# Spreading one expert's partial products over TensorE's four column groups, in a fused attention and soft-MoE kernel

## The chip, the cores and the metric

The kernel runs on one core of a Trainium2 chip. A core has TensorE (PE; its weight loads are listed apart as PEld), VectorE (DVE), ScalarE (ACT), GpSimd (POOL) and SyncE (SP), each with an instruction queue of its own that it works through in order, and 16 DMA engines that carry the transfers which SP and POOL issue. Matmuls write to PSUM; ScalarE and VectorE read it, GpSimd doesn't. The metric is the device time of one execution in microseconds (us). Inputs and output lie in HBM as float32.

## What is computed

Chunk-selected causal attention (4 batches, 8 heads, 768 positions, head size 64), whose output is the input of a soft mixture of experts: 3072 rows of 512 columns, 8 experts with 4 slots each, hidden size 1024. What matters here is the second part, cut from the reference:

```python
logits = x @ phi                                  # 3072 x 32
d = exp(logits - logits.max(0)); d /= d.sum(0)
slot_input = (d.T @ x).reshape(E, 4, 512)
for e in range(E):
    slot_out[e] = relu(slot_input[e] @ w1[e]) @ w2[e]
c = exp(logits - logits.max(1)); c /= c.sum(1)
return c @ slot_out.reshape(32, 512)
```

Every slot's output needs all rows of x, so nothing can be written before the last expert is done.

## The kernel before

**The loop.** 16 pairs of heads (4 per batch) are worked through by the loop from L570, i = 1 to 15; the order on each engine is the order in which the code issues the instructions. In step i stand the scores of pair i in six groups (`scores`, TensorE; L297 and L307), their exponentials (`expo`, ScalarE, L321) with causal masks (`mask`, GpSimd, L331), the products with v of pair i-1 (`pv`, L349), the normalisation and transposes of pair i-2 (L362, L371), and preparations for pairs i+1 and i+2 (transposes of k and q L205, bounds L256, selection L268). Scores have two PSUM buffers (`p_sc`), so ScalarE can be at most two groups behind TensorE.

**Loads.** All loads go through GpSimd's queue and are cast to bf16 on the way: k and q of pair i+4 (L145), v of pair i+2 (L150) and the sixteen expert matrices of 1 MB each (L138), spread over the steps by `wplan`. The last of the sixteen is w2 of expert 7.

**The MoE's part of the loop.** When the four pairs of a batch are done, the steps i = 6, 10 and 14 do that batch's share. Its combine weights are made in `moe_comb` (GpSimd, L457) and `moe_comb2` (L460): two exponentials on ScalarE write them to `c_pad`, a tile of 128 partitions x 6 row tiles x 4 groups x 32 columns. Expert e = 4g + j has columns 4g to 4g+3 of group j; columns 8 to 31 of each group stay zero from a memset at the start. `moe_ct` (L485) transposes `c_pad` on TensorE, six transposes (L488), and VectorE copies the result into `cT_all` (L496). In a step the order on GpSimd is: masks of groups 2 and 3, loads of k and q, rescaling of `si_acc` (`moe_scale`, L448, not for the first batch), load of v, load of a weight matrix, masks of group 4. On ScalarE the two exponentials of `moe_comb2` stand between the exponentials of groups 4 and 5. On TensorE `moe_ct` stands behind the last products with v of the step and ahead of the next step's scores.

**The tail.** The last batch's share follows from L653 on, with the same pieces. `experts_in` (L760) and `hidden_T` (L775) make the hidden layer. Slot outputs are summed in PSUM, `so_ps`, two halves of 256 columns each; group j (32 partitions) belongs to experts j and 4+j. `experts_out` (L795) multiplies: expert e uses one column group of TensorE, 32 columns of weights, so that matmuls of four experts can run side by side. Expert 7 comes last, alone. ScalarE copies both halves into `so_sb`, scaled by 1 over the column sums of d (`zinv`, from `zrow`); then `cT_all` times `so_sb` gives the output rows, which VectorE and ScalarE scale by 1 over the row sums of c (`cinv`, from `col_sums`, L679) on their way from PSUM, and SP stores them. The first 512 rows are made and stored in column halves (`half_out`, L827), the other 2560 at full width in pieces of 256 rows.

Of the kernel before, what the change touches and what calls it, by code (L numbers as in the profile page):

```python
# [10 lines left out]
F32 = mybir.dt.float32  # L11
BF16 = mybir.dt.bfloat16
ALU = mybir.AluOpType
ACT = mybir.ActivationFunctionType
# [4 lines left out]
CH = 32  # L19
NCHUNK = 24  # L20
NQT = 6
P = 128
# [38 lines left out]
def kernel(  # L61
# [23 lines left out]
    static = ctx.enter_context(tc.tile_pool(name="static", bufs=1))  # L85
# [13 lines left out]
    c_pad = static.tile([P, NQT, 4, CH], BF16, name="c_pad")  # L99
# [3 lines left out]
    w_sb = []  # L103
# [5 lines left out]
    ones_sq = static.tile([P, P], BF16, name="ones_sq")  # L109
# [4 lines left out]
    squad = static.tile([P, 2, 2, NCHUNK], BF16, name="squad")  # L114
    schunk = static.tile([P, 2, NCHUNK, 1], BF16, name="schunk")
    headsel = static.tile([P, 1, 2, 1], BF16, name="headsel")
    ns_t = [static.tile([P, NJ, 2, 2, CH], BF16, name=f"ns_t{i}") for i in range(2)]

    small = ctx.enter_context(tc.tile_pool(name="small", bufs=1))
# [43 lines left out]
        nc.vector.memset(t[:, :, :, D:D + 1], 1.0)  # L163
    for h in range(2):
        nc.vector.memset(headsel[h * 64:(h + 1) * 64, :, h, :], 1.0)

    nc.gpsimd.affine_select(
        out=squad, in_=squad, compare_op=ALU.not_equal, fill=NEG, base=0,
# [3 lines left out]
        out=squad, in_=squad, compare_op=ALU.not_equal, fill=-1.0, base=-NCHUNK,  # L172
# [5 lines left out]
        out=qgrp, in_=qgrp, compare_op=ALU.not_equal, fill=1.0, base=0,  # L178
# [3 lines left out]
        out=caus[:4], in_=caus[:4], compare_op=ALU.is_ge, fill=NEG, base=0,  # L182
# [277 lines left out]
    def moe_comb2(b):  # L460
        lc = st.pop(("lc", b))
        for g in range(2):
            nc.scalar.activation(
                c_pad[:, :, :, g * SPE:(g + 1) * SPE],
                lc[:, :, g * 16:(g + 1) * 16].rearrange("p t (j s) -> p t j s", j=4), func=ACT.Exp,
            )

    def moe_dispatch(b):
        d_sb = st.pop(("d", b))
        x = st.pop(("x", b)).rearrange("p t h d -> p t (h d)").rearrange("p t (a c x) -> p t a x c", a=NDG // 2, x=2)  # L470
        si = p_tp.tile([P, NDG + 1, NS], F32, name="si_ps", tag="tp")
        for dg in range(NDG + 1):
            for t in range(NQT):
                nc.tensor.matmul(
                    si[:, dg, :], lhsT=x[:, t, dg // 2, dg % 2, :] if dg < NDG else ones_sq,
                    rhs=d_sb[:, t, :], start=(t == 0), stop=(t == NQT - 1),
                )
        if b == 0:
# [173 lines left out]
    hT_pad = pads.tile([P, NFG, E, CH], BF16, name="hT_pad")  # L652
# [26 lines left out]
    def col_sums(ps, b):  # L679
        c = cT_all[:, b * NQT:(b + 1) * NQT].rearrange("p (m a) (c x) -> p m x (a c)", a=2, x=2)  # L680
        for n in range(NQT):
            nc.tensor.matmul(
                ps[:, n:n + 1], lhsT=c[:, n // 2, n % 2], rhs=ones_sq[:, :1], start=True, stop=True)

    csa = h_ps[0][:, 1, :BL * NQT]
    for b in range(BL):
# [18 lines left out]
    def cinv(n):  # L705
        return inv_a[:, n:n + 1] if n < BL * NQT else inv_b[:, 1 + n - BL * NQT:2 + n - BL * NQT]
# [4 lines left out]
        lg2, lhsT=mneg.broadcast_to([NS, P]), rhs=rep.broadcast_to([NS, NQT, NS]), start=False, stop=True,  # L711
# [3 lines left out]
        bc, lhsT=mneg.broadcast_to([NS, P]), rhs=identf[:NS, :NS], start=True, stop=True,  # L715
# [13 lines left out]
    for g in range(2):  # L729
        nc.scalar.activation(  # L730
            c_pad[:, :, :, g * SPE:(g + 1) * SPE],
            lc[:, :, g * 16:(g + 1) * 16].rearrange("p t (j s) -> p t j s", j=4), func=ACT.Exp,
        )
    keep(2)
    moe_dispatch(BL)
    keep(2)
# [2 lines left out]
    zrow = tail.tile([1, 4, CH], F32, name="zrow")  # L739
# [8 lines left out]
    for g in range(2):  # L748
        sl = slice(g * 16, (g + 1) * 16)
        nc.vector.tensor_tensor(  # L750
            zrow[:, :, g * SPE:(g + 1) * SPE],
            si_acc[:1, NDG, sl].rearrange("p (j s) -> p j s", j=4),
            si[:1, NDG, sl].rearrange("p (j s) -> p j s", j=4), op=ALU.add,
        )
    zinv = inv_b[:, :1]
    cT = cT_all.rearrange("p (m a) (c x) -> p m x (a c)", a=2, x=2)

    h_sb = tail.tile([P, 2, 512], BF16, name="h_sb")
    so_sb = [tail.tile([P, Dm // 2], BF16, name=f"so_sb{y}") for y in range(2)]
# [31 lines left out]
    HD = Dm // 2  # L791
    so_t = p_at.tile([P, 2, 512], F32, name="so_ps0", tag="at")
    so_ps = [so_t[:, 0, :HD], p_sc.tile([P, HD], F32, name="so_ps1", tag="sc")]

    def experts_out(fs, es, ys):  # L795
        for y, f in ((y, f) for y in ys for f in fs):
            for fg in range(f * 4, (f + 1) * 4):
                for e in es:
                    g, j = divmod(e, 4)
                    nc.tensor.matmul(  # L800
                        so_ps[y][j * CH:(j + 1) * CH, :], lhsT=hT_pad[:, fg, e, :],
                        rhs=w_sb[E + e][:, fg * Dm + y * HD:fg * Dm + (y + 1) * HD],
                        start=(g == 0 and fg == 0), stop=(g == 1 and fg == NFG - 1),
                    )

    experts_in(0, 0)
    moe_ct(B - 1)
# [3 lines left out]
    hidden_T(0)  # L811
    experts_in(1, 1)
    relu(1)
    NM, NH = B * NQT // 2, 2
    homes = {"sc": p_sc, "tp": p_tp, "at": p_at}
    half_homes = [iter("tp at sc tp".split()), iter("sc tp sc tp".split())]

    def rows(m):
        return out[m * 2 * P:(m + 1) * 2 * P, :].rearrange("(p x) d -> p x d", x=2)

    def scaled(x, o, ps, n):
        if x == 0:
            nc.vector.tensor_scalar_mul(o, ps, cinv(n))  # L823
        else:
            nc.scalar.activation(o, ps, func=ACT.Copy, scale=cinv(n))

    def half_out(m, y):  # L827
        o_sb = op.tile([P, 2, HD], F32, name="oh_sb", tag="oh_sb", bufs=2 * NH)
        for x in range(2):
            tag = next(half_homes[y])  # L830
            o_ps = homes[tag].tile([P, HD], F32, name="oh_ps", tag=tag)
            nc.tensor.matmul(o_ps, lhsT=cT[:, m, x], rhs=so_sb[y], start=True, stop=True)
            scaled(x, o_sb[:, x, :], o_ps, 2 * m + x)
            if m == y == 0:
                nc.sync.dma_start(out=rows(m)[:, x, :HD], in_=o_sb[:, x, :])
        if m + y > 0:
            nc.sync.dma_start(out=rows(m)[:, :, y * HD:(y + 1) * HD], in_=o_sb)

    w_ctx.close()
    op = ctx.enter_context(tc.tile_pool(name="op", bufs=5))  # L840
    experts_out([0], range(4), [0, 1])
    hidden_T(1)
    sums()
    experts_out([1], range(4), [0, 1])
    experts_out([0, 1], [4, 5, 6], [0, 1])
    experts_out([0, 1], [7], [0])
    nc.scalar.activation(so_sb[0], so_ps[0], func=ACT.Copy, scale=zinv)
    experts_out([0], [7], [1])
    half_out(0, 0)
    experts_out([1], [7], [1])  # L850
    nc.scalar.activation(so_sb[1], so_ps[1], func=ACT.Copy, scale=zinv)
    half_out(1, 0)
    for m in range(NH):
        half_out(m, 1)

    n = 0
    for m in range(NH, NM):
        o_sb = op.tile([P, 2, Dm], F32, name="o_sb", tag="o_sb")
        for x in range(2):
            tag = ("at", "sc", "tp", "sc", "tp")[n % 5]  # L860
            o_ps = homes[tag].tile([P, Dm], F32, name="o_ps", tag=tag)
            for y in range(2):
                nc.tensor.matmul(  # L863
                    o_ps[:, y * HD:(y + 1) * HD], lhsT=cT[:, m, x], rhs=so_sb[y], start=True, stop=True)
            scaled(x, o_sb[:, x, :], o_ps, 2 * m + x)
            n += 1
            if m == NM - 1:
                nc.sync.dma_start(out=rows(m)[:, x], in_=o_sb[:, x, :])
        if m < NM - 1:
            nc.sync.dma_start(out=rows(m), in_=o_sb)  # L870
# [30 lines left out]
```

## Time and profile before

| | |
|---|---|
| median of three runs | 166.99 us (166.96 to 167.58) |
| the profiled execution | 166.89 us, its span 165.2 us |
| busy share of the span: PE, DVE, ACT, POOL | 86%, 73%, 74%, 62% |
| moved on GpSimd's queue | 26.25 MB (bf16), read from HBM as float32 |
| stored on SP's queue | 6.29 MB |

How the lines are read: "start us, us, engine line op out<-in ... xcount [idle before <-releaser]" is one row of a timeline: when the first of the merged instructions started, how long from there to the end of the last, and, in brackets, how long the engine stood idle before it and what ended that. L331 is line 331 of the kernel. In the chain of waits a row is a stretch of the path that ended last. A row of windows has, for each engine, the busy time in that stretch and in brackets the number of instructions, then TensorE's granted clock (1.00 is full), the busy share of the DMA engines and GB/s. The page's strips cut the span into 40 slices of 4.13 us; digits are tenths. A busy TensorE isn't TensorE at its peak, since matmuls are pipelined.

### The profile page before, as it was taken

The numbers are of one execution on the slowest core, as the hardware profiler recorded it, in microseconds if no ns is written. First come the engines' busy times: TensorE is split into PE (matmuls) and PEld (weight loads), VectorE is DVE, ScalarE is ACT, GpSimd is POOL, SyncE is SP. The second block draws the span as 40 slices with busy tenths as digits, with TensorE's granted clock in tenths as the row PEclk, the third lists the DMA queues.
The fourth block names the chain that finished last, engine by engine and source line by source line (L and its number), as shares of the span: only waits on it lengthen the run. The fifth ranks groups of instructions, "written<-read, shape, count | busy, mean of one in ns | idle before, by whom it ended". The sixth has DMA issues, their size and how long they took to land.

```text
span 165.2 us, 6132 instructions
## 1 busy us (share of the span) xinstructions
PE 142.8 (86%) x2541; PEld 97.6 (59%) x2541; DVE 119.9 (73%) x419; ACT 122.8 (74%) x166; POOL 103.1 (62%) x202
## 2 busy tenths in 40 slices
PE   7986779999999898999999899998989999894500
PEld 2353456766767585677768567675868747552200
DVE  3376988989999979989997999898536521083620
ACT  3668879999999798999989699996886311193510
POOL 6978749979889398878949796768936200000000
PEclk9999999999999999999999999999999999999655
DMA  3999999999999999999999999999999999158995
GB/s 46 148 157 171 207 157 106 171 192 201 203 200 204 201 205 181 211 193 183 209 191 212 193 214 193 208 219 197 203 207 217 211 215 192 28 195 326 408 404 197
DMA packets 41132, 32.94 MB, mean 199 GB/s; under 512 B 26384, under 2 KB 35600, under 8 KB 41104
## 3 DMA queue, kind: packets, MB, share of 16 engines
q0 software_dynamic: 38416, 26.25, 108.0%
q1 hardware_dynamic: 2688, 6.29, 9.9%
q8 instruction: 20, 0.33, 0.7%
q14 instruction: 8, 0.07, 0.1%
HBM read 52.49 MB, written 6.29 MB: 356 GB/s over the span
## 4 chain that ended last, share of the span: by engine, by line
PE 31%; DMA 29%; ACT 18%; DVE 9%; issue 5%; POOL 4%; DVEq 0%; ACTq 0%
DMA w_sb<-in_moe_w_dram 14%; ACT e_sb L321 11%; DMA k_in<-in_k_dram 9%; DMA out_dram<-o_sb 6%; PE sc_ps L297 6%; PE at_ps L349 4%; PE tr_ps L205 4%; PE sc_ps L307 4%; PE warm_ps L197 4%; ACT qT L214 4%; PE xT_ps L371 2%; DVE mx L268 2%; PE ub_ps L256 2%; DVE x_sb L362 1%; POOL e_sb L331 1%
## 5 line engine op out<-in xcount | busy, mean ns | idle before, releaser
L321 ACT ACTIVATE e_sb<-sc_ps 128x1024 bf16<-128x1024 f32 (+1 forms) x96 | 83.1, 917 | 8.1 <-PE sc_ps L307 7.7
L331 POOL TENSOR_SCALAR_AFFINE_SELECT e_sb<-e_sb 128x256 bf16<-128x256 bf16 x96 | 38.4, 419 | 16.2 <-ACT e_sb L321 15.6
L297 PE MATMUL sc_ps<-qT,kT 64*128 64x384 bf16 (+3 forms) x258 | 36.8, 305 | 2.7 <-ACT e_sb L321 1.7
L307 PE MATMUL sc_ps<-nsT,smask 64*128 64x384 bf16 (+2 forms) x294 | 38.1, 284 | 0.1
L349 PE MATMUL at_ps<-v_t,e_sb 128*128 128x65 bf16 x672 | 29.9, 194 | 1.2 <-DVE x_sb L362 1.0
L349 PEld LDWEIGHTS <-e_sb 128*128 128x128 bf16 x672 | 25.4, 98 | 3.6 <-issue 2.1
L268 DVE MAX8 mx<-ub_ps 128x8 f32<-128x8 f32 (+1 forms) x192 | 17.0, 165 | 4.9 <-PE ub_ps L256 4.1
L297 PEld LDWEIGHTS <-kT 64*128 64x128 bf16 x258 | 14.0, 93 | 10.8 <-issue 5.4
L150 POOL DMA_DIRECT2D v_t<-in_v_dram x16 | 16.9, 1053 | 0.7 <-PE ns_ps L279 0.5
L307 PEld LDWEIGHTS <-smask 64*128 64x128 bf16 x294 | 14.9, 94 | 3.8 <-issue 0.6
L223 DVE TENSOR_REDUCE mm<-kT 128x24 bf16<-128x768 bf16 x16 | 15.1, 943 | 2.5 <-ACT kT L214 2.5
L362 DVE TENSOR_TENSOR x_sb<-at_ps,inv 128x768 bf16<-128x768 f32 (+1 forms) x17 | 15.5, 910 | 0.6
L229 DVE TENSOR_REDUCE mm<-kT 128x24 bf16<-128x768 bf16 x16 | 15.1, 943 | 0.0
L214 ACT COPY qT<-tr_ps 128x768 bf16<-128x768 bf16 x16 | 12.8, 800 | 2.5 <-PE tr_ps L205 2.5
L214 ACT COPY kT<-tr_ps 128x768 bf16<-128x768 bf16 x16 | 12.8, 801 | 1.5 <-PE tr_ps L205 1.5
L145 POOL DMA_DIRECT2D k_in<-in_k_dram x16 | 11.7, 734 | 1.1 <-POOLq L885 0.8
L145 POOL DMA_DIRECT2D q_in<-in_q_dram x16 | 11.5, 722 | 0.0
L138 POOL DMA_DIRECT2D w_sb<-in_moe_w_dram x16 | 11.4, 716 | 0.0
L382 DVE COPY xT_sb<-xT_ps 128x768 bf16<-128x768 bf16 (+1 forms) x15 | 8.1, 537 | 3.2 <-PE xT_ps L371 3.2
L863 PE MATMUL o_ps<-so_sb,cT_all 128*128 128x256 bf16 x40 | 6.8, 298 | 3.8 <-DVE o_sb L823 3.5
L205 PE MATMUL tr_ps<-ident,k_in 128*64 128x128 bf16 x192 | 8.7, 229 | 1.1 <-DMA k_in<-in_k_dram 1.1
L256 PE MATMUL ub_ps<-bd,qpn 128*128 128x48 bf16 x192 | 7.8, 183 | 1.3 <-DVE qpn L239 0.9
(125 smaller groups left out, 212.1 us busy)
## 6 DMA issues: line engine op xcount, KB each, us to landing
w_sb<-in_moe_w_dram POOLq DMA_DIRECT2D x16, 1024.0 KB, 14.0
out_dram<-o_sb SPq DMA_DIRECT2D x9, 512.0 KB, 5.3
k_in<-in_k_dram POOLq DMA_DIRECT2D x16, 192.0 KB, 7.0
q_in<-in_q_dram POOLq DMA_DIRECT2D x16, 192.0 KB, 7.3
v_t<-in_v_dram POOLq DMA_DIRECT2D x16, 192.0 KB, 8.5
out_dram<-oh_sb SPq DMA_DIRECT2D x3, 256.0 KB, 4.2
out_dram<-o_sb SPq DMA_DIRECT2D x2, 256.0 KB, 4.8
out_dram<-oh_sb SPq DMA_DIRECT2D x2, 128.0 KB, 1.9
```

The costliest lines, as they stand in the source:

```text
L145: nc.gpsimd.dma_start(out=t, in_=src.rearrange("h (p g) d -> p h (g d)", p=P))
L150: nc.gpsimd.dma_start(out=v_t[i % NV][:, :, :, :D], in_=v[b, 2 * j:2 * j + 2].rearrange("h (g p) d -> p h g d", p=P),)
L205: nc.tensor.matmul(ps[h * 64:(h + 1) * 64, g, :], lhsT=src[:, h, g * D:(g + 1) * D], rhs=ident, is_transpose=True,)
L214: nc.scalar.copy(t.rearrange("d (p g) -> d p g", g=NQT), st.pop((nm + "ps", i)).rearrange("d g p -> d p g"),)
L223: nc.vector.tensor_reduce(mm[:, 0, 0, :], kT, axis=AX.X, op=ALU.min)
L268: nc.vector.max(mx[:, a, :], ub[:, a, :max(8, 4 * t + 4)])
L297: nc.tensor.matmul(ps[:, h, c:c + w], lhsT=kT[r, kg * P:(kg + 1) * P], rhs=qT[r, qs], start=True, stop=False,)
L307: nc.tensor.matmul(ps[:, h, c + (f - t0) * P:c + (l - t0) * P], lhsT=smask[r, x, kg].rearrange("p a b -> p (a b)"), rhs=nsT[r, (f - x * NJ ...
L321: nc.scalar.activation(e[:, :, :w], st.pop(("scps", i, g))[:, :, :w], func=ACT.Exp, scale=scale)
L331: nc.gpsimd.affine_select(out=e[:, :, c:c + P], in_=e[:, :, c:c + P], compare_op=ALU.is_ge, fill=0.0, base=0, pattern=[[0, 2], [1, P]], ch ...
L349: nc.tensor.matmul(o, lhsT=st["e", i, g][:, h, c:c + P], rhs=v_t[i % NV][:, h, kg, :], start=(kg == 0), stop=(kg == t),)
L362: nc.vector.tensor_tensor(st["x", b][:, t0:t1, 2 * j:2 * j + 2, :].rearrange("p t h d -> p h t d"), at[:, :, :, :D], inv.broadcast_to([P, ...
```

## The change

Four edits, all around expert 7 and the stores:

1. Expert 7's eight matmuls of a half use the four column groups in turn (`last_expert_out`) instead of group 3 alone. The weights are taken from `hT_pad` four columns earlier, so that its four slots land in rows 8 to 11 of each group, and each group holds a quarter of the sum.
2. So that the combine adds the four quarters, expert 7's combine weights are copied to columns 8 to 11 of all four groups of `c_pad` (`spread_c`, on GpSimd, at the end of `moe_comb2` and once in the tail), and its sums of d likewise in `zrow`. Row sums of c are taken with `live`, which is 1 in rows 0 to 7 of each group and 0 elsewhere.
3. The first half of the slot outputs is copied by ScalarE, the second by VectorE.
4. Only the first 256 rows are made in column halves, and of these only the first 128 are stored in halves; buffers and engines of the full-width part are dealt out anew.

```diff
+    live = static.tile([P, 1], BF16, name="live")
...
+    nc.vector.memset(live, 0.0)
+    for j in range(4):
+        nc.vector.memset(live[j * CH:j * CH + 2 * SPE, :], 1.0)
...
     def moe_comb2(b):
...
+        spread_c()
+
+    def spread_c():
+        nc.gpsimd.tensor_copy(
+            c_pad[:, :, :, 2 * SPE:3 * SPE],
+            c_pad[:, :, 3:4, SPE:2 * SPE].broadcast_to([P, NQT, 4, SPE]))
...
-                ps[:, n:n + 1], lhsT=c[:, n // 2, n % 2], rhs=ones_sq[:, :1], start=True, stop=True)
+                ps[:, n:n + 1], lhsT=c[:, n // 2, n % 2], rhs=live, start=True, stop=True)
...
+    spread_c()
     keep(2)
     moe_dispatch(BL)
...
+    nc.gpsimd.tensor_copy(
+        zrow[:, :, 2 * SPE:3 * SPE], zrow[:, 3:4, SPE:2 * SPE].broadcast_to([1, 4, SPE]))
...
+    def last_expert_out(y):
+        h = hT_pad.rearrange("p f e c -> p f (e c)")[:, :, (E - 1) * CH - SPE:E * CH - SPE]
+        for fg in range(NFG):
+            j = fg % 4
+            nc.tensor.matmul(
+                so_ps[y][j * CH:(j + 1) * CH, :], lhsT=h[:, fg, :],
+                rhs=w_sb[2 * E - 1][:, fg * Dm + y * HD:fg * Dm + (y + 1) * HD],
+                start=False, stop=(fg >= NFG - 4),
+            )
...
     experts_out([0, 1], [4, 5, 6], [0, 1])
-    experts_out([0, 1], [7], [0])
+    last_expert_out(0)
     nc.scalar.activation(so_sb[0], so_ps[0], func=ACT.Copy, scale=zinv)
-    experts_out([0], [7], [1])
-    half_out(0, 0)
-    experts_out([1], [7], [1])
-    nc.scalar.activation(so_sb[1], so_ps[1], func=ACT.Copy, scale=zinv)
-    half_out(1, 0)
-    for m in range(NH):
-        half_out(m, 1)
+    last_expert_out(1)
+    nc.vector.tensor_scalar_mul(so_sb[1], so_ps[1], zinv)
+
+    first = op.tile([P, 2, Dm], F32, name="first", tag="o_sb")
+    half = {}
+    for y, tags in enumerate((("tp", "tp"), ("sc", "at"))):
+        for x in range(2):
+            half[x, y] = homes[tags[x]].tile([P, HD], F32, name="oh_ps", tag=tags[x])
+            nc.tensor.matmul(half[x, y], lhsT=cT[:, 0, x], rhs=so_sb[y], start=True, stop=True)
+    for x in range(2):
+        for y, scaled in enumerate((scaled_act, scaled_dve)):
+            cols = slice(y * HD, (y + 1) * HD)
+            scaled(first[:, x, cols], half[x, y], x)
+            if x == 0:
+                nc.sync.dma_start(out=rows(0)[:, x, cols], in_=first[:, x, cols])
+    nc.sync.dma_start(out=rows(0)[:, 1], in_=first[:, 1])
...
-    for m in range(NH, NM):
+    for m in range(1, NM):
...
-        for x in range(2):
-            tag = ("at", "sc", "tp", "sc", "tp")[n % 5]
+        for x, scaled in enumerate((scaled_act, scaled_dve)):
+            tag = ("sc", "tp", "tp", "sc", "at")[n % 5]
...
-            scaled(x, o_sb[:, x, :], o_ps, 2 * m + x)
+            scaled(o_sb[:, x, :], o_ps, 2 * m + x)
```

More of the change, by code (lines that the diff above doesn't have):

```diff
@@ L802, in experts_out @@
                         rhs=w_sb[E + e][:, fg * Dm + y * HD:fg * Dm + (y + 1) * HD],
-                        start=(g == 0 and fg == 0), stop=(g == 1 and fg == NFG - 1),
+                        start=(g == 0 and fg == 0), stop=False,
                     )
+    def last_expert_out(y):
[7 more added lines that the diff above has]
+            )
     experts_in(0, 0)
@@ L813, with scaled_act, scaled_dve @@
     relu(1)
-    NM, NH = B * NQT // 2, 2
+    NM = B * NQT // 2
     homes = {"sc": p_sc, "tp": p_tp, "at": p_at}
-    half_homes = [iter("tp at sc tp".split()), iter("sc tp sc tp".split())]
     def rows(m):
         return out[m * 2 * P:(m + 1) * 2 * P, :].rearrange("(p x) d -> p x d", x=2)
[L821 to L828, printed above, removed]
-        for x in range(2):
-            tag = next(half_homes[y])
-            o_ps = homes[tag].tile([P, HD], F32, name="oh_ps", tag=tag)
-            nc.tensor.matmul(o_ps, lhsT=cT[:, m, x], rhs=so_sb[y], start=True, stop=True)
-            scaled(x, o_sb[:, x, :], o_ps, 2 * m + x)
[L834 to L837, printed above, removed]
+    def scaled_act(o, ps, n):
+        nc.scalar.activation(o, ps, func=ACT.Copy, scale=cinv(n))
+    def scaled_dve(o, ps, n):
+        nc.vector.tensor_scalar_mul(o, ps, cinv(n))
     w_ctx.close()
@@ L845 @@
     experts_out([0, 1], [4, 5, 6], [0, 1])
-    experts_out([0, 1], [7], [0])
+    last_expert_out(0)
     nc.scalar.activation(so_sb[0], so_ps[0], func=ACT.Copy, scale=zinv)
-    experts_out([0], [7], [1])
-    half_out(0, 0)
-    experts_out([1], [7], [1])
-    nc.scalar.activation(so_sb[1], so_ps[1], func=ACT.Copy, scale=zinv)
-    half_out(1, 0)
-    for m in range(NH):
-        half_out(m, 1)
+    last_expert_out(1)
[13 more added lines that the diff above has]
+    nc.sync.dma_start(out=rows(0)[:, 1], in_=first[:, 1])
     n = 0
-    for m in range(NH, NM):
+    for m in range(1, NM):
         o_sb = op.tile([P, 2, Dm], F32, name="o_sb", tag="o_sb")
-        for x in range(2):
-            tag = ("at", "sc", "tp", "sc", "tp")[n % 5]
+        for x, scaled in enumerate((scaled_act, scaled_dve)):
+            tag = ("sc", "tp", "tp", "sc", "at")[n % 5]
             o_ps = homes[tag].tile([P, Dm], F32, name="o_ps", tag=tag)
@@ L864 @@
                     o_ps[:, y * HD:(y + 1) * HD], lhsT=cT[:, m, x], rhs=so_sb[y], start=True, stop=True)
-            scaled(x, o_sb[:, x, :], o_ps, 2 * m + x)
+            scaled(o_sb[:, x, :], o_ps, 2 * m + x)
             n += 1
```

## The prediction

> **What bounds the kernel now.** I read the page first, then the chain that ended last, then the timelines around the lines that the diff touches. All times are microseconds from the start of the profiled span. The page has two phases: weights and inputs come in on GpSimd's queue until about 142, and then 6.29 MB go out.
>
> ```profile
> PEclk9999999999999999999999999999999999999655
> DMA  3999999999999999999999999999999999158995
> GB/s 46 148 157 171 207 157 106 171 192 201 203 200 204 201 205 181 211 193 183 209 191 212 193 214 193 208 219 197 203 207 217 211 215 192 28 195 326 408 404 197
> ```
>
> The chain of waits around the seam, and TensorE's timeline there:
>
> ```profile
> 119.00 23.35 DMA w_sb<-in_moe_w_dram
> 142.36 0.04 issue
> 142.40 1.05 PE so_ps L800 x8
> ```
> ```profile
> 137.04 1.05 PE L800 MATMUL so_ps<-w_sb,hT_pad 128*32 128x256 bf16 x32
> 138.91 2.80 PE L800 MATMUL so_ps<-w_sb,hT_pad 128*32 128x256 bf16 x80
> 142.40 1.47 PE L800 MATMUL so_ps<-w_sb,hT_pad 128*32 128x256 bf16 x12 [0.69 <-DMA w_sb<-in_moe_w_dram]
> ```
>
> The last weight transfer lands at 142.36, 23.35 after its issue, so transfers are queued deep and a later issue would not make it land later. But TensorE came to that wait at 138.91 + 2.80 = 141.71. **The computation has only 0.69 in hand**: it and the weight stream are two nearly equal chains, and whatever delays the computation by more than 0.69 decides the end.
>
> **The change, part by part.**
>
> *Expert 7's products.* Eight matmuls in one column group took 1.05 (L800 x8); their first takes about 0.27, the rest 0.11 each. Over four groups 32 took 1.05 (the x32 row), so 0.025 each after the first: eight behind a running stream cost 8 x 0.025 = 0.20. Behind the weight wait they would end at 142.40 + 0.27 + 0.18 = 142.85, a gain of 0.60. If the groups did not overlap, they cost 0.8.
>
> *The copy that this needs.* Expert 7's partial sums lie in rows of all four groups, so its combine weights must be copied into those columns of c_pad. The copy stands on GpSimd, and the six transposes of c_pad, which waited for ScalarE's exponentials, now wait for it. GpSimd works in order, so I look at what it is doing at the three places inside the loop. First place (i=6):
>
> ```profile
> 61.19 1.04 POOL L150 DMA_DIRECT2D v_t<-in_v_dram  x1
> 61.21 0.46 ACT L463 ACTIVATE c_pad<-lc 128x96 bf16<-128x96 f32 x2
> 61.73 0.50 PE L488 MATMUL cT_ps<-ident,c_pad 128*128 128x128 bf16 x6
> 62.20 0.73 POOL L138 DMA_DIRECT2D w_sb<-in_moe_w_dram  x1
> 62.91 0.80 POOL L331 TENSOR_SCALAR_AFFINE_SELECT e_sb<-e_sb 128x256 bf16<-128x256 bf16 x2
> 64.17 0.53 PE L205 MATMUL tr_ps<-ident,k_in 128*64 128x128 bf16 x12 [0.44 <-DMA k_in<-in_k_dram]
> 65.72 1.51 ACT L321 ACTIVATE e_sb<-sc_ps 128x768 bf16<-128x768 f32 x2 [0.18 <-PE sc_ps L307]
> ```
>
> When TensorE wants c_pad at 61.73, GpSimd is still issuing a v and a weight transfer and then does the two masks of group 4, until 63.71. Only then comes the copy. The trace has no copy of 96 elements on GpSimd; the nearest rows bound it:
>
> ```profile
> 11.02 0.23 POOL L270 CAST ns_t<-mx 128x12 bf16<-128x12 f32 x1 [0.85 <-DVE mx L268]
> 117.69 0.52 POOL L448 TENSOR_TENSOR si_acc<-si_acc,dm 128x160 f32<-128x160 f32 x1
> ```
>
> Between 0.23 (12 elements) and 0.52 (160 elements, two inputs) I take 0.35, with 0.05 for the hand-over. The transposes then start at 64.11 and not at 61.73: **a stall of 2.38**. Behind them on TensorE stand the next pair's scores, for which ScalarE waits, and its transposes of k. What passes on: on TensorE the 0.44 wait for k_in is used up, 2.38 - 0.44 = 1.94; on ScalarE the 0.18, 2.20. I take 2.1.
>
> Second place (i=10), where a rescaling of si_acc stands ahead in the queue too:
>
> ```profile
> 90.54 1.07 POOL L150 DMA_DIRECT2D v_t<-in_v_dram  x1
> 91.61 0.70 POOL L138 DMA_DIRECT2D w_sb<-in_moe_w_dram  x1
> 92.32 0.78 POOL L331 TENSOR_SCALAR_AFFINE_SELECT e_sb<-e_sb 128x256 bf16<-128x256 bf16 x2
> 90.20 0.51 PE L488 MATMUL cT_ps<-ident,c_pad 128*128 128x128 bf16 x6
> 93.69 0.54 PE L349 MATMUL at_ps<-v_t,e_sb 128*128 128x65 bf16 x12 [0.61 <-DVE x_sb L362]
> 94.76 1.51 ACT L321 ACTIVATE e_sb<-sc_ps 128x768 bf16<-128x768 f32 x2 [0.84 <-PE sc_ps L307]
> ```
>
> Masks end at 93.10, the transposes start at 93.50, not at 90.20: **a stall of 3.30**. ScalarE uses up its 0.84 (2.46 left); TensorE its 0.61 (2.69), less a little where it was held up by VectorE in between. I take 2.45.
>
> Third place (i=14): no v load is left, only the two masks.
>
> ```profile
> 118.28 0.77 POOL L331 TENSOR_SCALAR_AFFINE_SELECT e_sb<-e_sb 128x256 bf16<-128x256 bf16 x2
> 118.71 0.39 PE L488 MATMUL cT_ps<-ident,c_pad 128*128 128x128 bf16 x4
> 119.79 3.35 ACT L321 ACTIVATE e_sb<-sc_ps 128x1024 bf16<-128x1024 f32 x4 [0.54 <-PE sc_ps L307]
> ```
>
> 119.05 + 0.40 = 119.45 and not 118.71: a stall of 0.74, and ScalarE, idle already, waits on. I take 0.7. In the last batch the copy has cover:
>
> ```profile
> 131.53 0.46 ACT L730 ACTIVATE c_pad<-lc 128x96 bf16<-128x96 f32 x2
> 133.54 0.51 PE L488 MATMUL cT_ps<-ident,c_pad 128*128 128x128 bf16 x6
> 133.30:140.40 7.10, 7.10 (x160) 4.75 (x155) 1.34 (x6) 1.19 (x2) 0.00 (x0) 1.00 1.00 201
> ```
>
> GpSimd is idle there, and 1.55 lie between the exponentials and the transposes; without that cover it would cost the 0.40. The same idle engine hides the copy of zrow. The five small memsets of `live` (about 0.09 each) lie in a 1.57 wait of VectorE for GpSimd at the start (row below), and the column sums only read another right-hand side: nothing.
>
> ```profile
> 2.35 0.17 DVE L165 MEMSET headsel<- 64x1 bf16 x2
> 4.09 0.18 DVE L187 TENSOR_TENSOR schunk<-squad 128x48 bf16<-128x48 bf16 x1 [1.57 <-POOL squad L171]
> ```
>
> In all **the computation comes 2.1 + 2.45 + 0.7 = 5.25 later**, at 141.71 + 5.25 = 146.96. The weights land long before that, so the 0.69 wait is gone and expert 7 follows straight on: its first half is summed at 146.96 + 0.20 = 147.16, against 142.40 + 1.05 = 143.45. That is +3.71.
>
> By a rule of the Trainium skill (GPSIMD Engine Reference, its introduction), GpSimd is the wrong engine for plain elementwise work, with VectorE about twice as fast. Halving the copies alone would give back 3 x 0.17, and the sum below would be 168.7; by the rows above most of each stall is the queue ahead of the copy, which the rule does not speak of.
>
> *The output.* From that point to the first store's issue the path has the same steps (an eviction, a 256-column matmul, an eviction). Behind it:
>
> ```profile
> 144.86 0.85 SPq L835 DMA_DIRECT2D out_dram<-oh_sb  x2
> 147.84 1.73 SPq L870 DMA_DIRECT2D out_dram<-o_sb  x1
> 152.65 0.75 DVE L823 TENSOR_SCALAR o_sb<-o_ps,inv_a 128x512 f32<-128x512 f32 x1 [2.70 <-DMA out_dram<-o_sb]
> ```
> ```profile
> 145.70:150.00 4.30, 4.04 (x30) 2.71 (x28) 4.17 (x7) 3.99 (x8) 0.00 (x0) 1.00 0.73 243
> 150.00:163.20 13.20, 3.02 (x14) 1.50 (x13) 3.76 (x5) 3.44 (x5) 0.00 (x0) 0.64 1.01 398
> ```
>
> While the half-width pieces went out, until 150.00, the stores ran at 243 GB/s, with one issue of 1.73 on the sync queue; afterwards at 398. After the change only 256 KB go in half columns. I put them 0.91 ahead of the rest (two issues, the L835 row's 0.85, and a hand-over), then 6291 - 256 = 6035 KB at 398 GB/s, 15.16; the stores took 163.2 - 145.7 = 17.5 and would take 16.07, a **gain of 1.43**. Bounds: nothing, if the sync queue stumbles again, to 4.30 - 4.30 x 243/398 = 1.67. The second slot-output copy, now on VectorE, is off this path: it starts with the second half's sums, in a wait. Five full-width output buffers instead of these and four half ones hold four transfers of 1.3 each (512 KB at 398 GB/s) in flight, and the two engines fill a buffer in 0.75, side by side: nothing.
>
> *Sum.* Against the profiled execution's 166.89 (span 165.2 and 1.69 around it; the median 166.99 is 0.10 above): 166.89 + 3.71 - 1.43 = **169.2**.
>
> **The rivals.**
>
> *Catching up (not slower).* If the delays pass on by less than 2.97, the gains cover them (141.71 + 2.97 + 0.20 - 143.45 = 1.43). The place would be ScalarE's idle time in the loop:
>
> ```profile
> ACT e_sb L321 <- PE sc_ps L307: 5.4, 11, 0.8
> ```
>
> Of these 5.4 (from 62 to 131), 1.4 are waits at the three places themselves (0.45, 0.45, 0.54), 1.8 I have used or come after the last (0.18, 0.84 and 0.74); about 2.2 are left. Were all of it used to catch up, 5.25 - 2.2 = 3.05 pass: 167.0. Were the computation hidden under the weights altogether, the time would be 166.89 - 0.60 - 1.43 = 164.9. Against it: those waits are for TensorE, which is late itself, and from 62 on no transfer but the k_in above holds the loop back.
>
> *The clock falls.* A stall of 3.30 empties TensorE. The trace shows one such fall:
>
> ```profile
> 153.46 0.82 PE L863 MATMUL o_ps<-so_sb,cT_all 128*128 128x256 bf16 x4 [2.85 <-DVE o_sb L823]
> 153.68:157.00 3.32, 2.19 (x10) 0.91 (x7) 2.12 (x3) 2.01 (x3) 0.00 (x0) 0.50 1.02 405
> ```
>
> After 2.85 of idling the granted clock was 0.50. How long it stays low under load no row shows; for as long as the stall itself, 3.3 at half speed cost 1.7: 170.9. By the Trainium skill (TensorE: Matmul & The Clock Gate, Part 1) the clock falls only after an idle window of about 3.4, on a grid that the program does not set; taken at its word a stall of 3.30 leaves it alone and the sum stands. The trace disagrees: it fell after 2.85.
>
> *The output gains nothing*: 169.2 + 1.4 = 170.6; for it speaks only that the 1.73 issue has no releaser shown. *The groups do not overlap*, so the new spread buys nothing: 169.8; the x32 row speaks against it.
>
> **How the numbers follow.** The sum 0.54, the fallen clock 0.22, catching up 0.14, no output gain 0.07, no overlap 0.03. The sum's own range is 168.2 to 170.3. Whole stalls with copies of 0.52 pass 6.93 on and give 170.9; with the clock's share I end the range at 171.4. Its low end is the 167.0 of catching up. A change under 0.5%, 166.16 to 167.83, could not be told from none: of catching up 0.08 lie there and 0.06 below. Slower has the rest, 0.86.
>
> **What would show it.** Right: the transposes of c_pad wait for GpSimd three times, by about 2.4, 3.3 and 0.7; ScalarE idles as long; TensorE no longer waits for the last weights, whose landing stays near 142.4; expert 7's first eight end about 0.2 after the stream before them; stores run near 400 GB/s from their third issue. Wrong: weights that land later, a wait for them that remains, or stalls that are gone two steps further on.

## The result, and the profile after

The changed kernel takes 172.9 us (median of four runs, 172.02 to 172.98) against 167.03 for the kernel before beside it (four runs, 166.96 to 167.58): a ratio of 1.033 [1.029, 1.037]. Slower was forecast, but 169.2, with a range that ends at 171.4. The profiled execution took 172.98, its span 171.3. (The profiled executions of two experiments, the loads behind the copy and the padding at the start, were 1.6% slower than the fastest runs of their kernels: their times come from the other runs, and their profiles are read only for waits, the order of the work, the granted clock and the stretch from the first sums to the end.)

The page's strips of the changed kernel, 40 slices of 4.28 us:

```profile
PEclk9999999999999996999999659999999999999755
GB/s 50 143 154 179 207 127 151 185 190 217 187 213 197 209 187 200 203 87 150 206 183 213 187 197 133 194 207 194 210 198 214 215 213 202 16 110 400 407 405 154
```

Two things are new against the strips of before. TensorE's granted clock dips in the 16th slice and in the 23rd and 24th; before, it was full until the stores. And the loads falter in the 18th and 25th slice (87 and 133 GB/s); the strip of before has 193 in both.

The timelines of GpSimd, TensorE and ScalarE at the three places inside the loop:

```profile
63.06 0.78 POOL L335 TENSOR_SCALAR_AFFINE_SELECT e_sb<-e_sb 128x256 bf16<-128x256 bf16 x2
63.78 0.26 POOL L474 COPY c_pad<-c_pad 128x96 bf16<-128x96 bf16 x1
64.10 0.51 PE L498 MATMUL cT_ps<-ident,c_pad 128*128 128x128 bf16 x6 [2.06 <-POOL c_pad L474]
66.73 0.85 PE L209 MATMUL tr_ps<-ident,k_in 128*64 128x128 bf16 x12
69.12 0.51 PE L375 MATMUL xT_ps<-ident,x_sb 128*128 128x128 bf16 x6
...
96.62 0.82 PE L498 MATMUL cT_ps<-ident,c_pad 128*128 128x128 bf16 x6 [3.10 <-POOL c_pad L474]
102.83 0.51 PE L375 MATMUL xT_ps<-ident,x_sb 128*128 128x128 bf16 x6
...
127.09 0.51 PE L498 MATMUL cT_ps<-ident,c_pad 128*128 128x128 bf16 x6 [0.44 <-POOL c_pad L474]
```

The transposes of c_pad (L498) wait for GpSimd's copy (L474) three times, by 2.06, 3.10 and 0.44. The copy itself takes 0.26; the masks ahead of it in GpSimd's queue end just as it starts. But look also at the rows behind the stalls: twelve transposes of k (L209) take 0.85, which took 0.53 before (the row at 64.17 in the prediction). Windows of 3.41 around the stalls, the granted clock being the third column from the end:

```profile
61.66:65.07 3.41, 1.35 (x28) 0.94 (x26) 1.61 (x4) 0.84 (x2) 2.38 (x5) 1.00 1.74 181
65.07:68.49 3.42, 3.42 (x49) 2.31 (x47) 2.79 (x17) 2.74 (x3) 1.28 (x4) 0.50 1.58 201
...
92.38:95.79 3.41, 1.14 (x43) 1.01 (x38) 1.76 (x5) 1.73 (x4) 3.39 (x6) 1.00 1.10 201
95.79:99.21 3.42, 2.59 (x21) 1.33 (x22) 1.65 (x3) 0.76 (x1) 0.78 (x3) 0.50 1.70 187
99.21:102.62 3.41, 3.41 (x47) 2.40 (x45) 2.38 (x14) 2.09 (x4) 2.18 (x5) 0.50 1.07 203
102.62:106.03 3.41, 3.41 (x69) 2.58 (x67) 2.57 (x8) 3.34 (x5) 2.58 (x5) 1.00 0.94 144
```

The clock is halved from 65.07 to 68.49 behind the first stall and from 95.79 to 102.62 behind the second. The first time it comes when the stall has been over for 0.97 (the transposes began at 64.10), and TensorE is busy for the whole window in which it runs slowly.

The seam, in the timelines of TensorE and ScalarE, and the DMA share (last column but one) of three windows:

```profile
145.43 1.05 PE L813 MATMUL so_ps<-w_sb,hT_pad 128*32 128x256 bf16 x32
147.29 2.58 PE L813 MATMUL so_ps<-w_sb,hT_pad 128*32 128x256 bf16 x74
149.61 0.28 PE L823 MATMUL so_ps<-w_sb,hT_pad 128*32 128x256 bf16 x1
150.37 0.47 ACT L857 ACTIVATE so_sb<-so_ps,inv_b 128x256 bf16<-128x256 f32 x1 [4.12 <-PE so_ps L823]
```
```profile
140.00:147.20 7.20, 7.20 (x143) 4.11 (x140) 1.87 (x10) 1.56 (x4) 0.59 (x3) 1.00 0.82 164
147.20:152.60 5.40, 5.03 (x115) 4.24 (x113) 1.86 (x5) 1.87 (x5) 0.00 (x0) 1.00 0.02 3
168.70:170.00 1.30, 0.00 (x0) 0.00 (x0) 0.00 (x0) 0.00 (x0) 0.00 (x0) 0.50 0.09 33
```

The first 32 slot-output matmuls start at 145.43 instead of 137.04, 8.39 later. Expert 7 (L823) waits for no transfer, and its first half is copied at 150.37 instead of 143.47, 6.90 later. From that copy to the end of the span it is 20.9 instead of 21.7. The last weights land at about 147.2, where the DMA share falls to 0.02, and not at 142.36. In the last 1.3 of the stores (168.7 to 170.0; the span ends 1.3 later) the DMA engines move 33 GB/s at a share of 0.09: little more than one of sixteen is still at work. So the loss of 6.1 is 6.9 lost ahead of the seam, less 0.8 gained behind it.

### The profile page after: what moved, and what is told of

Its sections match the earlier page's. It is cut to its first block, busy times and chain, and to the rows that moved or that the text cites. A ratio compares the mean times of both kernels' runs of the same rounds, so it can differ in the third digit from the quotient of the medians.

```text
span 171.3 us, 6140 instructions
## 1 busy us (share of the span) xinstructions
PE 144.8 (85%) x2541; PEld 98.8 (58%) x2541; DVE 121.3 (71%) x424; ACT 122.4 (71%) x164; POOL 104.3 (61%) x207
## 4 chain that ended last, share of the span: by engine, by line
PE 39%; DVE 16%; ACT 13%; DMA 13%; POOL 9%; issue 5%; DVEq 0%; ACTq 0%; SPq 0%
ACT e_sb L325 8%; DMA k_in<-in_k_dram 7%; PE sc_ps L301 6%; DMA out_dram<-o_sb 6%; PE tr_ps L209 5%; PE sc_ps L311 4%; PE at_ps L353 4%; PE warm_ps L201 4%; DVE mx L272 3%; POOL e_sb L335 3%; ACT qT L218 3%; PE xT_ps L375 2%; PE h_ps L779 2%; PE so_ps L813 2%; PE ub_ps L260 2%
## 5 line engine op out<-in xcount | busy, mean ns | idle before, releaser
L301 PE MATMUL sc_ps<-qT,kT 64*128 64x384 bf16 (+3 forms) x258 | 38.0, 315 | 2.8 <-ACT e_sb L325 1.9
L311 PE MATMUL sc_ps<-nsT,smask 64*128 64x384 bf16 (+2 forms) x294 | 39.2, 292 | 0.1
L209 PE MATMUL tr_ps<-ident,k_in 128*64 128x128 bf16 x192 | 9.4, 240 | 0.5 <-DMA k_in<-in_k_dram 0.5
```

The source lines that it names most:

```text
L209: nc.tensor.matmul(ps[h * 64:(h + 1) * 64, g, :], lhsT=src[:, h, g * D:(g + 1) * D], rhs=ident, is_transpose=True,)
L301: nc.tensor.matmul(ps[:, h, c:c + w], lhsT=kT[r, kg * P:(kg + 1) * P], rhs=qT[r, qs], start=True, stop=False,)
L311: nc.tensor.matmul(ps[:, h, c + (f - t0) * P:c + (l - t0) * P], lhsT=smask[r, x, kg].rearrange("p a b -> p (a b)"), rhs=nsT[r, (f - x * NJ ...
```

## The experiments

The theory at this point: the GpSimd copy alone causes the loss, by stalls of about 5.3 and by about 3 of half clock behind two of them. The rivals: late weights, or something in the new tail.

**The copy alone.** The kernel before with c_pad's copy on GpSimd and `live`; expert 7 and the stores as before (the copied columns meet zero rows there).

```diff
+    live = static.tile([P, 1], BF16, name="live")
...
+        spread_c()
...
-                ps[:, n:n + 1], lhsT=c[:, n // 2, n % 2], rhs=ones_sq[:, :1], start=True, stop=True)
+                ps[:, n:n + 1], lhsT=c[:, n // 2, n % 2], rhs=live, start=True, stop=True)
...
+    spread_c()
     keep(2)
```

> The kernel before with the copy of c_pad's columns on GpSimd alone (and the row sums with live). Theory: it carries the whole loss, 8.4 us of delay less the 0.69 us in hand, and none of the gains: 166.9 + 7.7 = 174.6 us, with the clock at half for some 10 us. Rival (part of the loss comes from the tail's edits): clearly less, 169 to 172 us.

> The kernel before, with only the copy on GpSimd (and live) added; expert 7 and the stores as before. The theory (stalls of 5.3 and 3.05 of half clock behind two of them, less the 0.69 of cover, nothing of it given back in the output): 7.7 above the kernel before, a ratio of about 1.046; half clock for about 3.4 and 6.8 behind the first and the second stall; the x32 row of the slot outputs near 145.5. The rival, that the new output part or expert 7's spread is itself a cause of the loss, would leave this kernel under 1.033, the ratio of the whole change.

The first run gave 173.13, the median of four times that lie too far apart (170.14 to 174.13) for a ratio; the second gave 172.84 against 167.32, a ratio of 1.036 [1.030, 1.042]. Its windows, the last of them from the first store on, and its seam:

```profile
61.28:64.69 3.41, 1.19 (x20) 0.81 (x20) 1.64 (x4) 0.43 (x2) 2.17 (x5) 1.00 1.73 181
64.69:68.10 3.41, 3.41 (x47) 2.26 (x45) 2.98 (x16) 2.64 (x3) 1.69 (x4) 0.50 1.65 200
95.41:102.23 6.82, 6.23 (x65) 3.73 (x65) 4.12 (x17) 3.08 (x4) 2.94 (x7) 0.50 1.37 200
152.35:156.62 4.27, 4.01 (x30) 2.70 (x28) 4.17 (x7) 3.95 (x8) 0.00 (x0) 1.00 0.89 309
```
```profile
144.93 1.04 PE L811 MATMUL so_ps<-w_sb,hT_pad 128*32 128x256 bf16 x32
150.09 0.47 ACT L858 ACTIVATE so_sb<-so_ps,inv_b 128x256 bf16<-128x256 f32 x1 [4.33 <-PE so_ps L811]
```

The one edit brings the whole loss: the same two stretches of half clock, and 7.89 at the x32 row (144.93 - 137.04). That is as the theory had it, and the rival, under 1.033, is not borne out. The expected 1.046 was too much, though: of the 7.89, 6.62 were left at so_sb (150.09 - 143.47), and the output, whose code is that of before, took 21.1 from there to the end of the span (171.2) instead of 21.7. In its first 4.27 the stores ran at 309 GB/s, where before's first 4.30 had 243.

**The stall filled.** The changed kernel with idle transposes of `ident` ahead of the real ones, about as many as the wait is long, so that TensorE is late but never idle.

```diff
     def moe_ct(b):
...
+        for n in range({0: 36, 1: 54, 2: 8}.get(b, 0)):
+            nc.tensor.matmul(ps[:, n % NQT, :], lhsT=ident, rhs=ident, is_transpose=True)
```

> The changed kernel with idle transposes of the identity ahead of the transposes of c_pad (36, 54 and 8, about 0.056 us each), so that TensorE is busy while it would wait. The stalls stay, the clock should not fall. Theory (of the 8.4 us delay, about 5.2 are the stalls and 3.2 the half clock behind them): 172.9 - 3.2 = 169.7 us, granted clock full until the stores. Rival (the half clock costs little, since ScalarE and VectorE set the pace of the loop, and the stalls cost more than I worked out): 172 to 173 us with a full clock.

168.35 (ten runs) against 167.66, a ratio of 1.004 [1.001, 1.007]; the profiled execution took 169.14, its span 167.4. Page and timelines:

```profile
PEclk9999999999999999999999999999999999999975
```
```profile
62.52 2.17 PE L498 MATMUL cT_ps<-ident 128*128 128x128 bf16 x36
64.75 0.51 PE L500 MATMUL cT_ps<-ident,c_pad 128*128 128x128 bf16 x6
68.52 0.50 PE L375 MATMUL xT_ps<-ident,x_sb 128*128 128x128 bf16 x6
96.01 0.51 PE L500 MATMUL cT_ps<-ident,c_pad 128*128 128x128 bf16 x6
99.78 0.50 PE L375 MATMUL xT_ps<-ident,x_sb 128*128 128x128 bf16 x6
142.38 1.05 PE L815 MATMUL so_ps<-w_sb,hT_pad 128*32 128x256 bf16 x32
147.32 0.47 ACT L859 ACTIVATE so_sb<-so_ps,inv_b 128x256 bf16<-128x256 f32 x1 [4.12 <-PE so_ps L825]
```

Useless work of the stall's length brings the ratio from 1.033 to 1.004, further down than the expected 169.7. The clock stays full to the stores. From the real transposes to the transposes of x (L375) it is 68.52 - 64.75 = 3.77 at both places, against 5.02 and 6.21 in the changed kernel: the half clock cost 1.25 and 2.44 on TensorE.

The x32 row stands at 142.38, 5.34 later than in the kernel before, where the changed kernel has 8.39. But the executions were not level when they came to the first stall. One row just ahead of it, in the kernel before, the changed kernel and this one:

```profile
61.20 0.30 PE L474 MATMUL si_ps<-d_sb,ones_sq 128*128 128x32 bf16 x6
61.34 0.30 PE L484 MATMUL si_ps<-d_sb,ones_sq 128*128 128x32 bf16 x6
61.99 0.30 PE L484 MATMUL si_ps<-d_sb,ones_sq 128*128 128x32 bf16 x6
```

The changed kernel was 0.14 late there and this one 0.79, before GpSimd's first copy of c_pad. The stalls alone therefore pass on 5.34 - 0.79 = 4.55, and the half clock 8.39 - 0.14 - 4.55 = 3.70, which agrees with 1.25 + 2.44. The filling has a second effect: its 98 additional matmuls move a fetch of instructions out of the stores (see the last experiment), and from so_sb to the end of the span it is 20.1 instead of 20.9. So not all of the gain from 1.033 to 1.004 is the clock's.

**Only the second and third stall filled.**

```diff
-        for n in range({0: 36, 1: 54, 2: 8}.get(b, 0)):
+        for n in range({1: 54, 2: 8}.get(b, 0)):
```

> As the run with filled stalls, but the first stall is left empty. Theory (the clock falls behind each stall that is left empty, and the fall behind the first, 3.4 us long, costs 1.0 us): the clock is at half once, for 3.4 us behind the first stall, and full behind the second; 1.0 us over the run with both filled, some 1.0 to 1.5% over the kernel before. Rival (only the longer, second stall costs): as the run with both filled, 0.4% over the kernel before.

169.44 (four runs) against 167.4, a ratio of 1.010 [1.004, 1.016]. In its windows and timeline:

```profile
61.95:65.36 3.41, 1.54 (x21) 0.93 (x22) 1.60 (x5) 0.57 (x2) 1.81 (x5) 1.00 1.75 181
65.36:68.77 3.41, 3.41 (x45) 2.28 (x43) 3.16 (x15) 2.59 (x4) 2.21 (x5) 0.50 1.57 204
```
```profile
63.82 0.51 PE L500 MATMUL cT_ps<-ident,c_pad 128*128 128x128 bf16 x6 [2.21 <-POOL c_pad L474]
68.88 0.51 PE L375 MATMUL xT_ps<-ident,x_sb 128*128 128x128 bf16 x6
```

One stretch of half clock is left, where it was. From the real transposes to the transposes of x it is 68.88 - 63.82 = 5.06 here, 1.29 more than with the stall filled. The medians differ by 169.44 - 168.35 = 1.1, near the expected 1.0, but they come from two sets of runs and the intervals of the ratios overlap; it is the trace that speaks against the rival. Of the 3.7 of half clock some 1.3 are the first stall's, and the larger part is the second's.

**The loads behind the copy.** The changed kernel, but in steps 6, 10 and 14 the v and weight transfers are issued after the copy and not ahead of it.

```diff
-        if have(i + 2):
+        if have(i + 2) and not slots:
...
-        if i < EARLY:
+        if i < EARLY and not slots:
...
+        if have(i + 2) and slots:
+            load_v(i + 2)
+        if i < EARLY and slots:
+            weights(i)
```

> The changed kernel; only in the three steps with a batch's share, the v and weight loads (1.03 and 0.71 us of GpSimd) are issued behind the copy of c_pad instead of ahead of it. Theory (the stall is GpSimd's queue ahead of the copy): the stalls shrink from 2.06, 3.10 and 0.44 to about 0.5, 1.4 and 0.5 us, none is long enough to bring the clock down, about 1.7 us of delay pass on, 0.69 of them covered: 0.5 to 1 us under the kernel before, with the granted clock full until the stores. Rival (the place in the queue matters little, the copy itself or its hand-over costs): within 1 us of the changed kernel.

167.05 (ten runs) against 167.4, a ratio of 0.997 [0.994, 1.001]. Timelines, and one window:

```profile
62.61 0.37 POOL L474 COPY c_pad<-c_pad 128x96 bf16<-128x96 bf16 x1
63.04 0.51 PE L498 MATMUL cT_ps<-ident,c_pad 128*128 128x128 bf16 x6 [0.66 <-POOL c_pad L474]
92.83 0.51 PE L498 MATMUL cT_ps<-ident,c_pad 128*128 128x128 bf16 x6 [1.63 <-POOL c_pad L474]
145.26 0.62 PE L827 MATMUL so_ps<-w_sb,hT_pad 128*32 128x256 bf16 x16 [1.25 <-DMA w_sb<-in_moe_w_dram]
```
```profile
90.94:94.35 3.41, 1.78 (x30) 1.05 (x27) 2.00 (x6) 1.27 (x3) 3.40 (x7) 1.00 1.10 193
```

Moving two issues past a copy of 0.37 gives back the loss: the stalls are 0.66 and 1.63, the clock does not fall behind either, and the time is level with the kernel before. In the profiled execution the weights now decide: expert 7 waits 1.25 for them.

**The copy on ScalarE.** Columns 8 to 11 are written by a third exponential from the same logits, in ScalarE's place in the order, with nothing on GpSimd.

```diff
-    def spread_c():
-        nc.gpsimd.tensor_copy(
+    def spread_c(lc):
+        nc.scalar.activation(
             c_pad[:, :, :, 2 * SPE:3 * SPE],
-            c_pad[:, :, 3:4, SPE:2 * SPE].broadcast_to([P, NQT, 4, SPE]))
+            lc[:, :, 7 * SPE:8 * SPE].rearrange("p t (j s) -> p t j s", j=1).broadcast_to([P, NQT, 4, SPE]),
+            func=ACT.Exp,
+        )
```

> Theory (the whole loss is TensorE's wait for GpSimd's late copy, and the two falls of the clock that follow from it): with the third slice of c_pad written by ScalarE straight behind its two exponentials, nothing waits for GpSimd, the 8.4 us of delay are gone, the clock falls nowhere before the stores, the weights bind again at about 142.4, and the gains of the tail are left: 166.9 - 0.6 - (0.8 to 1.4) = 164.9 to 165.5 us. Three more exponentials of about 0.2 us on ScalarE lie in the 0.69 us in hand. Rival (the loss lies in the tail's edits or elsewhere): 170 us or more, as in the changed kernel.

> The kernel with the copy on ScalarE once more, to stand beside the next one on the same chip: 1% under the kernel before, one DMA engine 1.2 to 1.3 us behind the others in the stores, from the transfer in which a 16 KB instruction packet falls.

> The copy on ScalarE again, beside the padded kernel on the same chip: ratio 0.986 to 0.989, one engine 1.2 to 1.3 behind the others at the end.

Three runs, on three occasions: ratios of 0.989 [0.984, 0.994], 0.986 [0.981, 0.991] and 0.996 [0.993, 1.000]. The medians were 166.11, 164.86 and 166.14. It beats the changed kernel by far, and the kernel before by 1.1%, 1.4% and 0.4%, the third time by less than expected and with an interval that reaches 1.000. The timelines of TensorE and ScalarE in the first of the three:

```profile
142.64 0.62 PE L825 MATMUL so_ps<-w_sb,hT_pad 128*32 128x256 bf16 x16 [1.38 <-DMA w_sb<-in_moe_w_dram]
143.09 0.47 ACT L859 ACTIVATE so_sb<-so_ps,inv_b 128x256 bf16<-128x256 f32 x1 [5.67 <-PE so_ps L825]
```

The computation waits 1.38 for the last weights, and 0.45 after they are there the first half is summed (143.09 - 142.64), where one column group took 1.07 (143.47 - 142.40).

**The tail alone.** The changed kernel's sums, copies and stores, but expert 7 in one column group and no copies on GpSimd.

```diff
     def spread_c():
-        nc.gpsimd.tensor_copy(
-            c_pad[:, :, :, 2 * SPE:3 * SPE],
-            c_pad[:, :, 3:4, SPE:2 * SPE].broadcast_to([P, NQT, 4, SPE]))
+        pass
...
     def last_expert_out(y):
...
+        experts_out([0, 1], [7], [y])
```

> The changed kernel without the spread: expert 7 in one column group, no copy of c_pad or zrow. Theory: the store edits alone gain 0.8 to 1.4 us and the weights bind: 165.5 to 166.1 us; against the run with the copy on ScalarE it misses the 0.6 us of the four column groups. Rival (the store edits gain nothing, the tail's shortening in the changed kernel came from expert 7 alone): 166.9 us.

166.29 (six runs) against 167.66: 0.990 [0.985, 0.994]. The expected times, 0.992 to 0.995 of 166.89, lie for the most part within the interval, and the rival's 166.9 doesn't. How much of it is the stores' stays open. In the profiled execution, with a span of 163.9, expert 7 waits for the weights until 141.63 and so_sb is copied from 142.70, 0.77 earlier in both than in the kernel before, which no edit here explains: the same wait ends at 142.64, 141.47 and 143.00 in the three runs with ScalarE's copy. Only the rest is the output's: 21.2 from so_sb to the end of the span and not 21.7.

**The fetch moved.** In the last 1.3 of the changed kernel's stores little more than one DMA engine was still at work, and a packet of the instruction queue falls among its stores. Its DMA queues between 154.4 and 155.9 (packets, MB, share of 16 engines):

```profile
q1 hardware_dynamic: 160, 0.59, 98.5%
q8 instruction: 1, 0.02, 5.6%
```

5.6% of 16 engines over 1.5 are 1.34 on one engine. If the packet belongs to TensorE's program, more instructions ahead of it make it come earlier. Two kernels with ScalarE's copy and 44 one-column matmuls, first ahead of expert 7, then at the very start in place of seven of nine warming matmuls:

```diff
+    pad_ps = p_tp.tile([P, 1], F32, name="pad_ps", tag="tp")
+    for _ in range(44):
+        nc.tensor.matmul(pad_ps, lhsT=ident, rhs=ones_sq[:, :1], start=True, stop=True)
     last_expert_out(0)
```
```diff
-    warm(9)
+    for _ in range(44):
+        nc.tensor.matmul(warm_ps[:, 0, :1], lhsT=ones_sq, rhs=ones_sq[:, :1], start=True, stop=True)
+    warm(2)
```

> As before with 44 matmuls of one column more on TensorE (1 us, in its wait for the last weights), which only move the instruction stream on. Theory (the store that lands last is held up by the packet of instructions that one DMA engine fetches for TensorE in the middle of the stores): the packet falls ahead of the first store, the last engine ends 0.5 to 0.6 us behind the others and not 1.3, and the time is 0.6 to 0.8 us under the run beside it. Rival (the engine that lags does so by itself): the same lag, and the same time or a little more.

> The copy on ScalarE, with 44 one-column matmuls in place of seven of the nine warming matmuls at the very start of TensorE's queue. The theory that TensorE's instruction count decides when its next instructions are fetched: the fetch between 142 and 148 comes 44 instructions earlier in TensorE's order, before the first store, so no DMA engine ends more than 0.6 behind the median one, the output phase from the first sums to the last packet takes 18.8 and not 19.5, and, as the padding costs nothing here, the time is 0.6 below the same kernel without it: a ratio of about 0.983 to the kernel before. The rival, that the straggling engine has another cause: a lag of 1.2 as before and a ratio of 0.986 to 0.989.

The first took 165.66 (eleven runs; 0.991 [0.988, 0.994]), 0.8 more than the same kernel without it on that occasion (164.86): the padding lasted from 140.96 to 142.88, 1.92 and not 1.0, and expert 7 waited for it and no longer for the weights. The second took 165.64 (0.992 [0.988, 0.996]) beside 166.14 for the same kernel without it: 0.5 less where 0.6 was expected, but the intervals overlap, and both ratios lie above those expected. In both traces the packet has moved as expected: it falls at 143.74 and 144.02, ahead of the first store at 145.58 and 147.48. The last 1.3 of the stores, in the kernel unpadded (the run beside the second) and padded at the start; padded ahead of expert 7, the share and the rate are those of the second row:

```profile
161.80:163.10 1.30, 0.00 (x0) 0.00 (x0) 0.00 (x0) 0.00 (x0) 0.00 (x0) 0.50 0.38 147
```
```profile
162.80:164.10 1.30, 0.00 (x0) 0.00 (x0) 0.00 (x0) 0.00 (x0) 0.00 (x0) 0.50 0.53 205
```

The engines end closer together, and from so_sb to the end of the span it is 20.2 in both padded kernels (143.34 to 163.5, 145.23 to 165.4) against 21.0 (143.45 to 164.4). With the stalls filled, where the fetch also fell ahead of the first store, it was 20.1 (147.32 to 167.4). So the output is shorter by 0.8 where the fetch is out of it; that the times follow isn't shown beyond the noise.

## Why the prediction was right, and where it was wrong

| term | predicted | changed kernel | stalls filled, full clock |
|---|---|---|---|
| passed on by the three stalls | 5.25 | 4.55 | 4.55 |
| passed on by the half clock | 0 | 3.70 | 0 |
| late already ahead of the first stall | 0 | 0.14 | 0.79 |
| start of the x32 row | +5.25 | +8.39 | +5.34 |
| first half of the slot outputs | +3.71 | +6.90 | +3.85 |
| output, from there to the end | -1.43 | -0.81 | -1.65 |
| the profiled execution | 169.2 | 172.98 | 169.14 |

The 4.55 and the 3.70 are those worked out from the run with the stalls filled.

**The step that failed is the choice to let the clock stay full** and to make its fall a rival with a chance of 0.22, priced once, at 1.7, behind the second stall. It fell behind both, for 3.4 and 6.8, and this passed on 3.70. The prediction had the warning row before it (0.50 after 2.85 of idling) and used it for one stall, with the stall's own length as the time at half speed; the time at half speed was in fact one window of 3.41 behind 2.06 of idling and two behind 3.10.

That the rest of the sum comes out is in part luck. 169.2 + 3.7 is the 172.9 measured, but the stalls passed on 0.70 less than taken, and the output gave back 0.62 less. In the last column 169.14 stands beside 169.2 because that execution was 0.79 late from the start and its output gained 0.2 more than predicted, which makes up for the stalls; by the ratio, 1.004 x 166.89, that kernel takes 167.6.

**The stalls** were right in place and cause: 2.06, 3.10 and 0.44 against 2.38, 3.30 and 0.74, smaller in part by the copy's 0.26 where 0.35 was taken. Of the 5.60 they pass on 4.55, the same share as the prediction took (5.25 of 6.42). That the queue ahead of the copy is the price, not the copy, is borne out by the loads behind the copy. By the Trainium skill (GPSIMD Engine Reference, its introduction) VectorE is roughly twice as fast at ordinary elementwise arithmetic. If that held for this copy, it would by estimate take 0.13 and not 0.26, and save 0.4 in all, of a loss of 6; no run here shows it.

**The weights** were wrong but decided nothing: a later issue does make them land later, at 147.2 and not near 142.4. Late weights were among the prediction's own signs of being wrong. Behind the first stall GpSimd issued a load of v and one of a weight matrix at 77.63 and 78.66, where the kernel before has 74.38 and 75.40, and between 74.5 and 77 the transfers had run dry:

```profile
74.50:77.00 2.50, 2.50 (x50) 1.83 (x50) 2.47 (x13) 2.46 (x5) 2.17 (x5) 1.00 0.47 43
```

The quoted 23.35 from issue to landing did not mean that much in hand all along. In the profiled execution with the loads behind the copy the late weights became the bound.

**Expert 7** was right: behind the running stream its first half ended within 0.28 (the eighty matmuls before it began at 147.29 and take 2.80 as before, so_sb was copied from 150.37), 0.20 predicted. Where the weights bind, ScalarE's copy shows the gain of 0.6 (0.45 against 1.07). Only its worth behind a running stream was less than the rival without overlap had it, 0.2 and not 0.6: from the x32 row to so_sb it is 4.94 in the changed kernel, 5.16 in the copy alone, where expert 7 has one group.

**The output** was mis-sized: 0.81 and not 1.43. The second failed step is to have read the gain from one execution of before, as if the slow start of its stores, with an issue of 1.73 on the sync queue, would be gone. The changed kernel has such an issue too:

```profile
155.16 1.62 SPq L889 DMA_DIRECT2D out_dram<-o_sb  x1
```

In both kernels it comes with a fetch of instructions among the stores (from 147.98 and from 154.48); that the fetch makes the issue long isn't shown. The copy alone runs the store code of before, at 309 GB/s and not 243 in the half-width part, and takes 21.1; the changed kernel's 20.9 is then only 0.2 better. Where the fetch falls ahead of the stores, the gain over the kernel before is 1.6. What the tail's edits are worth on top of the copy stays open: the ratios, 1.036 ± 0.006 and 1.033 ± 0.004, differ by 0.003 ± 0.007, a gain of anything up to 1.6.

**Catching up** by 2.2 did not happen: at full clock the stalls passed on the share that the sum had taken.

## What to carry to other kernels

Before a small operation goes to an in-order engine, read what that engine has queued ahead of it at that moment, and who waits: here 0.26 of copying cost 6, and hardly anything once two loads were issued after it and not before, or the engine that made its input did it. A stall of TensorE has two prices, its length and the half clock behind it; read the busy share of the windows around it, and price the second with the first. Before the same row of two executions is compared, take off how far apart they were ahead of the first place that the edit touches: here 0.65 between two of them. Read a gain in the stores from more than one execution.

## What the runs showed of the hardware

**The clock changes on a fixed grid, behind windows with little work.** In these traces the granted clock changes only on a grid of 3.413 us: in the changed kernel at 65.07, 68.49, 95.79 and 102.62 (95.79 - 65.07 is nine such windows). A window with TensorE busy for 1.35, 1.14, 1.19 or 1.54 of 3.41 (33 to 45%) was followed by half clock; one with 1.78 (52%, the loads behind the copy) was not. A sharp border in busy time the traces do not give: among the stores a window with 1.87 (55%, from 146.36 in the tail alone) was followed by half clock too. At half clock a window busy for 2.59 of 3.42 (76%) was followed by another slow one, a fully busy one by full clock. By the Trainium skill (TensorE: Matmul & The Clock Gate, Part 1) the clock falls after an idle window of about 3.4 on a free-running grid; the traces agree on the grid and its length, but a window did not have to be idle throughout: one that was busy for 45% was followed by half clock. If the busy share of such a window decides, a stall of about 2 costs a slow window or nothing by where it lies on the grid; that it would be spared in another place was not tried.

**A fetch of instructions among the stores goes with a longer output.** One packet of 16 KB took 1.34, and little more than one engine was left in the last 1.3 of the stores; that it is the engine that carried the packet is read from the times alone. 44 more matmuls on TensorE ahead of it moved it out of the stores, and the output then took 0.8 less (20.2 and not 21.0).
